# A drain of GpSimd's queue, independent scatters and a later load at the end of an attention and mixture-of-experts kernel

## The chip, the cores and the metric

The kernel runs on one core of one Trainium2 chip. The metric is the device time of one execution in microseconds (us), as the median of several runs; lower is better. The core has five engines with queues of their own: TensorE (PE, with its weight loads as PEld), VectorE (DVE), ScalarE (ACT), GpSimd (POOL) and SyncE (SP), which issues most transfers. A "q" behind an engine's name (POOLq, SPq) means instructions that its queue handles itself, such as waits on semaphores, register loads, branches and drains.

## The reference

Bucketed attention over 4 batches of 8 heads with 768 tokens of width 64 (a query sees the keys whose six sign bits agree with its own), and behind it a mixture of experts on the 3072 tokens of width 512. Each token goes to the one of 8 experts that scores highest:

```python
logits = x @ w_gate + modality_bias[modality_id]
e_idx = np.argmax(logits, axis=1)
...
for e in range(E):
    mask = e_idx == e
    h = np.maximum(x[mask] @ w1[e], 0.0)
    out[mask] = gate_w[mask, None] * (h @ w2[e])
```

Each row of `out` is thus written once, by the expert of its token.

## The kernel before

Attention runs first, over 16 pairs of heads. It leaves x in device memory (`x_d`), and a router writes, with indirect scatters on GpSimd (line 607), a table `tab` in which the tokens are sorted by expert, with their gate weights.

The experts then work in slots. A big slot (kinds "e" and "b") holds 512 tokens of one expert, in four groups of 128; a small one (kind "s") holds up to 128. The order is e0, e1, b0, b1, s1, b2, b3, s0: the last slot is a small one, and a big one precedes it. Within a slot, GpSimd gathers the tokens from `x_d` (line 770), TensorE multiplies by w1 (steps j = 0 to 3) and w2 (j = 4 to 7) with weights that SP loads and ACT and DVE split into two parts (lines 742 to 752), and at the slot's end `store` (line 849) does two things for each group of 128 tokens: ACT scales the result out of PSUM into a tile `y` (line 852; four buffers), and GpSimd scatters `y` to the rows of `out` that the table names (line 853).

The rows of a scatter are known at run time only. The framework that orders the instructions therefore takes two scatters to `out` as two writes of the same tensor, and puts a wait in front of each: GpSimd holds the next scatter until the one before it has landed.

For the case that an expert has more tokens than the eight slots hold, `conditional` follows (line 931). Every engine loads the flag `tot[0:1, 2:3]` into a register (line 941) and branches on it (line 942); with these inputs the flag is 0 and the body is skipped. An engine that skips the body raises the semaphores that the body would have raised (single event-semaphore instructions on each engine and, on GpSimd, one INC_SWDGE_SEM for those of its transfers). After that comes the framework's own end of the program, which the profile books under line 994: SP waits on the semaphores, each engine has a DRAIN, and all meet at a barrier. The kernel has no drain of its own. The program's begin is booked under line 991.

Instructions of one engine run in the order of its queue. In the slots from the third on that order is the framework's; `tc.issue_after(ins)` keeps what is inside it behind `ins` on the engine of `ins` alone, and `tc.declare_no_dep` takes the dependence between two instructions away.

Of the kernel before, what the change touches and what calls it, by code (L numbers as in the profile page):

```python
# [490 lines left out]
N = B * S  # L491
# [221 lines left out]
def experts(ctx, tc, a, x_d, tab, out, ps_x, ident, first, adds):  # L713
    nc = tc.nc
# [14 lines left out]
    def nt(s):  # L729
        return 1 if s[0] == "s" else TG  # L730
# [61 lines left out]
    def gemm1(hi, lo, xh, xl, hh, hl):  # L792
        hi = hi.rearrange("p (c f) -> p c f", c=4)
        lo = lo.rearrange("p (c f) -> p c f", c=4)
        for fb in range(2):
            fs = slice(fb * P, (fb + 1) * P)
            hps = ps_h.tile([P, TS], F32, name="hps")
            for c in range(4):
                nc.tensor.matmul(hps, lo[:, c, fs], xh[:, c], start=(c == 0), stop=False)  # L799
                nc.tensor.matmul(hps, hi[:, c, fs], xl[:, c], start=False, stop=False)  # L800
                nc.tensor.matmul(hps, hi[:, c, fs], xh[:, c], start=False, stop=(c == 3))  # L801
            th = hp.tile([P, TS], F32R, name="hh")
            tl = hp.tile([P, TS], F32R, name="hl")
            with tc.high_priority(offset=CFG["hpo"]):
                nc.scalar.activation(th, hps, AF.Relu)  # L805
                nc.vector.scalar_tensor_tensor(out=tl, in0=hps, scalar=0.0, in1=th.bitcast(F32), op0=ALU.max, op1=ALU.subtract)  # L806
            hh.append(th)
            hl.append(tl)
            if fb == 0:
                yield  # L810

    def gemm1_small(hi, lo, xh, xl):
        hi = hi.rearrange("p (c f) -> p c f", c=4)
        lo = lo.rearrange("p (c f) -> p c f", c=4)
        hps = ps_h.tile([P, TS], F32, name="hps")[:, 0:FW]
        for c in range(4):
            nc.tensor.matmul(hps, xh[:, c, 0:P], lo[:, c], start=(c == 0), stop=False)
            nc.tensor.matmul(hps, xl[:, c, 0:P], hi[:, c], start=False, stop=False)
            nc.tensor.matmul(hps, xh[:, c, 0:P], hi[:, c], start=False, stop=(c == 3))
        h = hp.tile([P, FW], F32, name="hn", bufs=2)  # L820
        nc.scalar.activation(h, hps, AF.Relu)
        return h

    def turn_small(h, hh, hl):
        tp = ps_h.tile([P, TS], F32, name="hps")[:, 0:FW]
        for fb in range(2):
            nc.tensor.transpose(tp[:, fb * P:(fb + 1) * P], h[:, fb * P:(fb + 1) * P], ident)
        th = hp.tile([P, TS], F32R, name="hh")[:, 0:FW]
        tl = hp.tile([P, TS], F32R, name="hl")[:, 0:FW]
        nc.scalar.copy(out=th, in_=tp)  # L830
        nc.vector.tensor_tensor(out=tl, in0=tp, in1=th.bitcast(F32), op=ALU.subtract)
        for fb in range(2):
            hh.append(th[:, fb * P:(fb + 1) * P])
            hl.append(tl[:, fb * P:(fb + 1) * P])

    def gemm2(j, hi, lo, hh, hl, yps):
        hi = hi.rearrange("p (c f) -> p c f", c=2)
        lo = lo.rearrange("p (c f) -> p c f", c=2)
        for fb in range(2):
            fc = (j - 4) * 2 + fb  # L840
            for g in range(len(yps)):
                gs = slice(g * P, (g + 1) * P)
                nc.tensor.matmul(yps[g], hl[fc][:, gs], hi[:, fb], start=(fc == 0), stop=False)  # L843
                nc.tensor.matmul(yps[g], hh[fc][:, gs], lo[:, fb], start=False, stop=False)  # L844
                nc.tensor.matmul(yps[g], hh[fc][:, gs], hi[:, fb], start=False, stop=(fc == 7))  # L845
            if fb == 0:
                yield

    def store(tb, yps):
        for g in range(len(yps)):  # L850
            y = yp.tile([P, DM], F32, name="y")
            nc.scalar.activation(y, yps[g], AF.Copy, scale=tb[:, g, 1:2].bitcast(F32))  # L852
            nc.gpsimd.indirect_dma_start(out=out, out_offset=bass.IndirectOffsetOnAxis(ap=tb[:, g, 0:1], axis=0), in_=y, in_offset=None,  # L853
                                         bounds_check=N - 1, oob_is_err=False)

    class Runner:


        def __init__(self):
            self.raws, self.ws, self.got, self.xs = {}, {}, {}, {}  # L860
            self.nl = self.ns = self.n = 0
            self.seq, self.order = [], []

        def extend(self, lst):
            self.order += lst
            self.seq += [(s, j) for s in lst for j in range(8)]
# [25 lines left out]
        def slot(self, k):  # L892
            s = self.order[k]
            nxt = self.order[k + 1] if k + 1 < len(self.order) else None
            for _ in self.prepare(s):
                pass
            hh, hl, h = [], [], None
            ready = self.prepare(nxt) if nxt else iter(())
            for j in range(8):
                self.ahead()  # L900
                if j == (2 if k == 1 else 0) and k > 0:
                    for s2 in self.order[k + 1:k + 1 + CFG["fd"]]:
                        self.fetch(s2)
                if j == 4:
                    yps = [ps_y.tile([P, DM], F32, name="yps") for _ in range(nt(s))]
                    if k != 1:
                        for n, _ in enumerate(ready):
                            if k == 0 and n == 0:
                                break
                hi, lo = self.ws.pop(self.n)  # L910
                if j >= 4 or nt(s) > 1:
                    for _ in gemm2(j, hi, lo, hh, hl, yps) if j >= 4 else gemm1(hi, lo, *self.xs[s], hh, hl):
                        if k == 0 and j >= 4 or k == 1 and j >= 6:
                            next(ready, None)
                        yield
                    if k == 0 and j >= 4 or k == 1 and j >= 6:
                        next(ready, None)
                else:
                    last, h = h, gemm1_small(hi, lo, *self.xs[s])
                    if last is not None:  # L920
                        turn_small(last, hh, hl)
                if j == 4 and h is not None:
                    turn_small(h, hh, hl)
                self.n += 1
                yield
            store(self.got[s][0], yps)

    def conditional(tot):
        def rest(kind, i, n, col):
            if i == n:  # L930
                return
            t = nc.values_load(tot[0:1, col:col + 1], min_val=0, max_val=16, skip_runtime_bounds_check_because="a count of slots") if i in (SURE_BIG, SURE_SML) else rest.t
            rest.t = t
            with tc.If(t > i):
                r = Runner()
                r.extend([(kind, i)])
                for _ in r.slot(0):
                    pass
                rest(kind, i + 1, n, col)

        more = nc.values_load(tot[0:1, 2:3], min_val=0, max_val=1, skip_runtime_bounds_check_because="0 or 1")  # L941
        with tc.If(more > 0):
            rest("b", SURE_BIG, NBIG, 0)
            rest("s", SURE_SML, NSML, 1)
# [5 lines left out]
def body(tc, a, out):  # L950
# [3 lines left out]
    with ExitStack() as ctx, ExitStack() as actx:  # L954
        route, early_slots, early_tables, early_tiles, late_slots, setup, latest, adds, bias = router(ctx, tc, a, x_d, tab)
        finish, finish_x, ps_x, ident = attention(ctx, actx, tc, a, x_d, route, setup, early_slots, early_tables, latest, adds, bias)
        actx.close()
        runner, tabs, conditional = experts(ctx, tc, a, x_d, tab, out, ps_x, ident, early_tiles, adds)
        r = runner()
        r.extend([("e", i) for i in range(EARLY)])  # L960
# [37 lines left out]
```

## Time and profile before

| | us |
|---|---|
| median of 3 runs (lowest, highest) | 808.18 (806.52, 808.47) |
| the profiled execution | 806.52 |
| its span, from first to last instruction | 804.5 |
| TensorE busy | 751.0 (93%) |
| DVE, ACT, POOL busy | 501.7, 413.4, 438.9 |

The profiled execution is the quickest of the three runs; 2.02 us of its time lie outside the span. Times in the rows are us from the span's start. A row of the timeline gives start, duration, engine, line and operation, and in brackets the idle time of the engine before it with what ended that. Register, branch, semaphore and drain instructions don't count as busy: a stretch at the end in which all engines show zero can still hold such instructions, and they are found by their line.

### The profile page before, as it was taken

Reading aid. Unit: us, or ns where it says so; the run is one execution under the profiler, and the core shown is the slowest. Engines: PE = TensorE matmul, PEld = TensorE weight load, DVE = VectorE, ACT = ScalarE, POOL = GpSimd, SP = SyncE. Lnnn points to the kernel's source line nnn. Section 1 sums busy time; section 2 is a strip of 40 time slices with the busy share of each in tenths; the row PEclk is TensorE's granted clock in tenths of the full one; section 3 lists DMA queues with packets and bytes.
Section 4 is the critical chain, followed back from the end, with each engine's and each line's share of the span. In section 5 each row is a group of like instructions: output and inputs, shape, how many; then the busy total and the mean of one; then the engine's idle time right before and its main releaser. Section 6 shows DMA issues by size and latency. Waiting matters only on the chain. (4 is left out here: it accounts for less than half of the span.)

```text
span 804.5 us, 11625 instructions
## 1 busy us (share of the span) xinstructions
PE 751.0 (93%) x4060; PEld 520.6 (65%) x4060; DVE 501.7 (62%) x839; ACT 413.4 (51%) x730; POOL 438.9 (55%) x321
## 2 busy tenths in 40 slices
PE   4899999999998999999899999999999999999993
PEld 2555566555565556565556546888888888888882
DVE  6787677578778669778769857744243334643420
ACT  3566676666646666666556455333343436533340
POOL 7198889778869777879866992123220103202011
PEclk9999999999999999999999999999999999999997
DMA  6665534343356543456221547475443446733310
GB/s 205 151 177 158 143 98 133 99 125 106 108 121 154 134 121 92 135 127 147 72 59 34 149 75 262 121 129 197 157 132 96 140 118 212 259 103 127 122 50 37
DMA packets 59573, 104.24 MB, mean 130 GB/s; under 512 B 9709, under 2 KB 30829, under 8 KB 59504
## 3 DMA queue, kind: packets, MB, share of 16 engines
q1 hardware_dynamic: 53424, 88.23, 39.9%
q0 software_dynamic: 4928, 13.14, 5.1%
q10 hardware_dynamic: 1152, 2.03, 0.8%
q8 instruction: 34, 0.56, 0.3%
q14 instruction: 35, 0.29, 0.2%
HBM read 59.89 MB, written 13.33 MB: 91 GB/s over the span
## 5 line engine op out<-in xcount | busy, mean ns | idle before, releaser
L295 POOL TENSOR_TENSOR sp<-sp,pb 128x768 f32<-128x768 f32 x124 | 232.2, 1895 | 14.2 <-ACT pb L292 12.9
L285 ACT ACTIVATE pb<-pss 128x512 f32<-128x512 f32 x192 | 114.1, 598 | 110.5 <-PE pss L274 101.1
L219 DVE TENSOR_REDUCE mx<-psm 128x1 f32<-128x512 f32 x192 | 130.4, 687 | 55.8 <-PE psm L217 54.2
L752 DVE TENSOR_TENSOR w<-raw,w 128x1024 fp32r<-128x1024 f32 x64 | 79.5, 1249 | 94.3 <-ACT w L750 85.5
L319 PE MATMUL psu<-pb,vt 128*64 128x512 f32 (+1 forms) x768 | 134.4, 492 | 0.0
L750 ACT CAST w<-raw 128x1024 fp32r<-128x1024 f32 x64 | 66.9, 1050 | 73.8 <-PE yps L845 62.5
L319 PEld LDWEIGHTS psu<-pb,vt 128*64 128x64 f32 x768 | 50.8, 136 | 69.1 <-issue 58.3
L295 POOL TENSOR_TENSOR sp<-pb,pb 128x768 f32<-128x768 f32 x31 | 58.9, 1921 | 54.5 <-ACT pb L292 38.1
L273 PE MATMUL pss<-a_0g 128*128 128x512 f32 x192 | 79.7, 415 | 5.4 <-ACT pb L285 3.9
L843 PE MATMUL yps<-w,hl 128*128 128x512 f32 x208 | 82.7, 398 | 0.0
L845 PE MATMUL yps<-w,hh 128*128 128x512 f32 x208 | 81.3, 391 | 0.0
L844 PE MATMUL yps<-w,hh 128*128 128x512 f32 x208 | 81.0, 389 | 0.0
L799 PE MATMUL hps<-xh,w 128*128 128x512 f32 x192 | 75.6, 394 | 0.3 <-DVE hl L806 0.2
L800 PE MATMUL hps<-xl,w 128*128 128x512 f32 x192 | 74.9, 390 | 0.5 <-DVE xl L789 0.5
L801 PE MATMUL hps<-xh,w 128*128 128x512 f32 x192 | 74.9, 390 | 0.0
L225 DVE TENSOR_REDUCE mx<-psm 128x2 f32<-128x512 f32 x96 | 66.2, 690 | 10.7 <-PE psm L223 9.0
L273 PE MATMUL pss<-a_1g 128*128 128x512 f32 x192 | 68.8, 358 | 3.7 <-ACT pb L292 3.7
L770 POOL DMA_INDIRECT xg<-x_d,tb x18 | 21.3, 1186 | 91.8 <-DMA tb<-tab 84.1
L853 POOL DMA_INDIRECT out<-y,tb x18 | 19.1, 1062 | 93.4 <-ACT y L852 48.0
L805 ACT ACTIVATE hh<-hps 128x512 fp32r<-128x512 f32 x48 | 28.7, 598 | 74.5 <-PE hps L801 73.3
L806 DVE SCALAR_TENSOR_TENSOR hl<-hps,hh 128x512 fp32r<-128x512 f32 x48 | 33.0, 688 | 52.6 <-ACT hh L805 51.9
L274 PE MATMUL pss<-b_0g 128*128 128x512 f32 x192 | 65.5, 341 | 0.0
(203 smaller groups left out, 1413.6 us busy)
## 6 DMA issues: line engine op xcount, KB each, us to landing
raw<-moe_w SPq DMA_DIRECT2D x64, 512.0 KB, 4.4
xt<-qk SPq DMA_DIRECT2D x31, 384.0 KB, 4.4
vt<-v SPq DMA_DIRECT2D x16, 384.0 KB, 7.2
a_0g<-hx SPq DMA_DIRECT2D x30, 192.0 KB, 3.5
a_1g<-hx SPq DMA_DIRECT2D x30, 192.0 KB, 3.8
x_d<-xs SPq DMA_DIRECT2D x18, 256.0 KB, 2.0
b_1g<-a_1g SPq DMA_DIRECT2D x17, 192.0 KB, 3.1
b_0g<-a_0g SPq DMA_DIRECT2D x17, 192.0 KB, 2.7
```

The lines of the kernel that those rows point to most:

```text
L219: newest[:] = [nc.vector.tensor_reduce(out=mx[:, qt + j, 1 - h, 0:1], in_=mp, axis=AX.X, op=ALU.max).ins]
L273: nc.tensor.matmul(out, t["s1"][h][:, ks], t["m1"][h][:, cs], start=True, stop=False)
L285: nc.scalar.activation(t["pb"][kt][:, h, 0:MAIN], sp, AF.Exp, scale=0.125)
L295: add = (nc.vector if h and i in CFG["spd"] else nc.gpsimd).tensor_tensor(out=t["sp"][:, h], in0=(t["pb"][0] if kt == 1 else t["sp"])[:, h ...
L319: nc.tensor.matmul(t["u"][part][64 * h:64 * h + 64, 0:w], t["v"][:, h, kt], t["pb"][kt][:, h, COLS[part]], start=False, stop=(kt == NT - 1 ...
L752: (nc.gpsimd if pool else nc.vector).tensor_tensor(out=lo, in0=r, in1=hi.bitcast(F32), op=ALU.subtract)
L799: nc.tensor.matmul(hps, lo[:, c, fs], xh[:, c], start=(c == 0), stop=False)
L800: nc.tensor.matmul(hps, hi[:, c, fs], xl[:, c], start=False, stop=False)
L801: nc.tensor.matmul(hps, hi[:, c, fs], xh[:, c], start=False, stop=(c == 3))
L843: nc.tensor.matmul(yps[g], hl[fc][:, gs], hi[:, fb], start=(fc == 0), stop=False)
L844: nc.tensor.matmul(yps[g], hh[fc][:, gs], lo[:, fb], start=False, stop=False)
L845: nc.tensor.matmul(yps[g], hh[fc][:, gs], hi[:, fb], start=False, stop=(fc == 7))
```

## The change

Three edits. Scatters to `out` from the eight sure slots are declared independent of each other, so that GpSimd no longer waits for one to land before it issues the next. In the last slot, at j = 4, a `drain` is put on GpSimd's queue behind the last scatter of the slot before; only the last scatter is still to come. And the load of the flag is kept behind the last scatter on GpSimd's queue. Runners of the conditional body are made with `sure=False` and keep their waits.

```diff
+    stored = []
+
+    def store(tb, yps, sure):
...
+            ins = nc.gpsimd.indirect_dma_start(out=out, out_offset=bass.IndirectOffsetOnAxis(ap=tb[:, g, 0:1], axis=0), in_=y, in_offset=None,
+                                               bounds_check=N - 1, oob_is_err=False).ins
+            for other in stored:
+                tc.declare_no_dep(ins, other, reason="every token is in one slot and has its own row of out")
+            if sure:
+                stored.append(ins)
...
+                if j == 4 and self.sure and k == len(self.order) - 1:
+                    with tc.issue_after(stored[-1]):
+                        nc.gpsimd.drain()
...
-                r = Runner()
+                r = Runner(False)
...
-        more = nc.values_load(tot[0:1, 2:3], min_val=0, max_val=1, skip_runtime_bounds_check_because="0 or 1")
+        with tc.issue_after(stored[-1]):
+            more = nc.values_load(tot[0:1, 2:3], min_val=0, max_val=1, skip_runtime_bounds_check_because="0 or 1")
```

## Rows read from the trace of the kernel before

**Rows 1.** The page, part 1: busy us, share and instructions of two engines.

```profile
PE 751.0 (93%) x4060; PEld 520.6 (65%) x4060; DVE 501.7 (62%) x839; ACT 413.4 (51%) x730; POOL 438.9 (55%) x321
```

**Rows 2.** Busy time by stretch: length, PE, PEld, DVE, ACT, POOL, clock, DMA share, GB/s.

```profile
540.00:790.00 250.00, 249.56 (x1185) 207.89 (x1184) 102.70 (x116) 101.66 (x146) 47.31 (x42) 1.00 0.44 141
...
793.00:794.00 1.00, 0.00 (x0) 0.00 (x0) 0.00 (x0) 0.00 (x0) 0.00 (x0) 1.00 0.48 193
794.00:795.00 1.00, 0.00 (x0) 0.00 (x0) 0.00 (x0) 0.00 (x0) 0.00 (x0) 1.00 0.08 25
...
796.00:797.00 1.00, 0.00 (x0) 0.00 (x0) 0.00 (x0) 0.00 (x0) 0.00 (x0) 0.50 0.00 0
```

**Rows 3.** Timeline of GpSimd from 770 us on: the last five scatters.

```profile
776.83 0.98 POOL L853 DMA_INDIRECT out<-y,tb  x1 [28.40 <-ACT y L852]
780.27 1.37 POOL L853 DMA_INDIRECT out<-y,tb  x1 [2.46 <-ACT hn L821]
784.04 0.98 POOL L853 DMA_INDIRECT out<-y,tb  x1 [2.39 <-ACT hh L830]
787.46 0.98 POOL L853 DMA_INDIRECT out<-y,tb  x1 [2.44 <-ACT hh L830]
791.92 0.98 POOL L853 DMA_INDIRECT out<-y,tb  x1 [3.48 <-ACT y L852]
```

**Rows 4.** The chain that ended last, in order of time: start, us, what.

```profile
787.46 3.69 DMA out<-y,tb
...
791.18 0.02 POOLq L853
...
791.72 0.50 POOLq L941
```

**Rows 5.** Line 942, 791 to 798 us: duration min/median/max in ns, starts.

```profile
L942 POOLq EVENT_SEMAPHORE  x5: 17/43/43, 795.2 to 795.5; - x5
...
L942 POOLq COMPARE_BRANCH  x1: 53/53/53, 792.3 to 792.3; - x1
L942 POOLq INC_SWDGE_SEM  x1: 1708/1708/1708, 795.6 to 795.6; - x1
```

**Rows 6.** Line 994, the end of the program, the same view.

```profile
L994 SPq EVENT_SEMAPHORE  x14: 17/28/28, 797.2 to 804.4; - x14
...
L994 POOLq DRAIN  x3: 40/107/6286, 797.3 to 804.2; - x3
```

**Rows 7.** Line 994 again, 797.5 to 803 us alone: SP's drains.

```profile
L994 SPq DRAIN  x2: 7/10/13, 798.4 to 798.4; - x2
```

**Rows 8.** Waits of SP from 500 us on: us in total, times, longest.

```profile
SPq L994 <- DMA out<-y,tb: 28.2, 1, 28.2
```

**Rows 9.** Timeline of ACT: the y of the last two slots.

```profile
775.86 1.37 ACT L852 ACTIVATE y<-yps,tb 128x512 f32<-128x512 f32 x2 [2.35 <-PE yps L845]
...
790.68 0.69 ACT L852 ACTIVATE y<-yps,tb 128x512 f32<-128x512 f32 x1 [3.76 <-PE yps L845]
```

**Rows 10.** Timeline of GpSimd, 515 us on: second of six scatters without waits.

```profile
519.86 1.00 POOL L607 DMA_INDIRECT tab<-recs,posi  x1 [0.31 <-issue]
```

**Rows 11.** The DMA view: issues from GpSimd's queue.

```profile
tab<-recs,posi POOLq DMA_INDIRECT x24
xg<-x_d,tb POOLq DMA_INDIRECT x18
out<-y,tb POOLq DMA_INDIRECT x18
...
xg<-x_d,ete POOLq DMA_INDIRECT x8
out<-y,etb POOLq DMA_INDIRECT x8
```

**Rows 12.** Line 991, the program's begin: GpSimd's queue.

```profile
L991 POOLq INC_SWDGE_SEM  x1: 27/27/27, 0.1 to 0.1; - x1
...
L991 POOLq DRAIN  x1: 188/188/188, 0.3 to 0.3; - x1
```

More of the change, by code (lines that the diff above doesn't have):

```diff
@@ L847, in gemm2 @@
                 yield
-    def store(tb, yps):
+    stored = []
+    def store(tb, yps, sure):
         for g in range(len(yps)):
@@ L852, in store, with __init__ @@
             nc.scalar.activation(y, yps[g], AF.Copy, scale=tb[:, g, 1:2].bitcast(F32))
-            nc.gpsimd.indirect_dma_start(out=out, out_offset=bass.IndirectOffsetOnAxis(ap=tb[:, g, 0:1], axis=0), in_=y, in_offset=None,
-                                         bounds_check=N - 1, oob_is_err=False)
+            ins = nc.gpsimd.indirect_dma_start(out=out, out_offset=bass.IndirectOffsetOnAxis(ap=tb[:, g, 0:1], axis=0), in_=y, in_offset=None,
[4 more added lines that the diff above has]
+                stored.append(ins)
     class Runner:
-        def __init__(self):
+        def __init__(self, sure=True):
             self.raws, self.ws, self.got, self.xs = {}, {}, {}, {}
@@ L862, in __init__ @@
             self.seq, self.order = [], []
+            self.sure = sure
         def extend(self, lst):
@@ L925, in slot @@
                 yield
-            store(self.got[s][0], yps)
+            store(self.got[s][0], yps, self.sure)
     def conditional(tot):
```

## The prediction

> **What bounds the kernel now.** I first read the page's busy times: TensorE is busy for 93% of the span [rows 1]. Next comes the table of busy time by stretch, to see whether that share is even. In the expert stage from 540 to 790 us TensorE is busy 249.56 of 250 us, so its own stream sets the time there, and GpSimd, busy 47.31 us, has room [rows 2]. The reader should see that nothing GpSimd does earlier or later in that stretch can shorten it; what is left is the tail. The last y is made on ACT from 790.68 to 791.37 [rows 9], and the span ends at 804.5, so 13.1 us pass in which no TensorE work remains.
>
> The timeline shows only one scatter in that tail [rows 3]; the rest are queue instructions, which I read by line. In order: GpSimd's wait for the scatter before ends at 791.20 and the flag's load runs 791.72 to 792.22 [rows 4]; the last scatter starts at 791.92 [rows 3]; GpSimd branches at 792.3, its next instructions come at 795.2, and INC_SWDGE_SEM takes 795.6 to 797.3 [rows 5]. Then a DRAIN of 6.29 us starts at 797.3 [rows 6] and ends at 803.59; 0.91 us of closing barrier follow. SP is done long before: its waits begin at 797.2 [rows 6, 8] and its drains stand at 798.4 [rows 7]. So the chain that sets the end is GpSimd's queue, and its largest piece is the drain.
>
> What does that drain do? No transfer is its cause: the last scatter's bytes move between 793 and 794 us, and the DMA share is 0.00 from 796 us on [rows 2]. The drain at the program's begin, with no transfer issued yet, took 0.19 us, and the two shorter ones at the end, right behind the long one, 0.04 and 0.11 us [rows 12, 6]. So a long drain comes once, the first time after 24 + 18 + 18 + 8 + 8 = 76 indirect transfers [rows 11], and those behind it are short. My reading: GpSimd's software closes the books on each transfer since the last drain, at an estimated 6.29 / 76 = 0.083 us each.
>
> A rule speaks against this. The Trainium skill, "VectorE: DVE Perf Modes", section "The DRAIN you can't avoid", says that the drains of the preamble and postamble are about 12 ns, constant, on all five engines. SP's rows (7 to 13 ns) fit it [rows 7], GpSimd's 6286 ns doesn't. By its "constant" the last drain would keep its length whatever went before; that is the first rival below, which stands on rows alone.
>
> **The change, part by part.** *Independent scatters.* They take away the waits between scatters. In the last big slot four scatters start at 776.83, 780.27, 784.04 and 787.46, about 3.5 us apart [rows 3]. All four y are ready by 775.86 + 4 x 0.69 = 778.62 [rows 9], and scatters without waits follow each other in 0.31 + 1.00 = 1.31 us, as the table's do [rows 10]. So they will start at 776.83, 778.1, 779.5 and 780.8 and leave GpSimd at 781.7. Earlier in the stage the same edit gains nothing, as TensorE's own 249.56 us cover it [rows 2]. If that cover were absent, a gather behind a waiting scatter would start some us sooner. More scatters in flight beside the weight loads cost nothing I can point to at a DMA share of 0.44 [rows 2].
>
> The last scatter no longer waits for the one before, only for its y. The first scatter of the big slot shows that case: y ends at 775.86 + 0.69 = 776.55, the scatter starts at 776.83, 0.28 later [rows 9, 3]. By that the last one starts at 791.37 + 0.28 = 791.65 in place of 791.92: **-0.27 us**.
>
> *The early drain.* It stands behind the fourth scatter on GpSimd's queue. Behind it are the last scatter, the flag's load and the branch; nobody else waits for them before the end. It has 75 transfers to close, 75 x 0.083 = 6.2 us. No row shows a drain beside other work, so I bound its end: 781.7 + 6.2 = 787.9 if it closes old transfers while the last ones land, and, with the longest landing of a scatter in the chain, 3.69 us [rows 4], 780.8 + 3.69 + 6.29 = 790.8 at the latest if it waits for all landings first. GpSimd is needed again at about 791.6. The cover is TensorE's last slot, with 0.8 to 3.7 us to spare, so the cost on the path is 0. I lean to the first end, since 71 of the 75 have landed long ago.
>
> *The load behind the last scatter.* In the trace it starts at 791.72, after the wait that stands ahead of the scatter, so it already is behind it [rows 4]; with the waits gone, the edit keeps it there. **0 us**, and at most its 0.50 us in either direction.
>
> *INC_SWDGE_SEM* isn't edited, but works on the same queue. It took 1.71 us with 76 transfers open and will meet one [rows 5, 11]. At the program's begin it took 0.03 us [rows 12]. I bound it by 0.03 and 1.71 and take 0.3, near the lower end, because the begin's state (nothing open) is nearer to one open transfer than 76 are: **-1.41 us**.
>
> *The last drain.* It has one transfer to close, so I take the program begin's 0.19 us [rows 12]. Then it is no longer the last: INC_SWDGE_SEM starts at 795.6 - 0.27 = 795.33 and ends at 795.63, GpSimd's drain ends at 795.8. SP comes late next. Its 28.2 us wait ended at 797.2, 0.1 before INC_SWDGE_SEM's end [rows 8, 6, 5] and well after the bytes had moved, so I read that instruction as its releaser. From there SP's list of waits took 1.2 us to its drains [rows 7]. So SP is through at 795.53 + 1.2 = 796.73, and 0.91 us of closing give 797.64. From INC_SWDGE_SEM's end to the span's end that is 2.01 us where it was 7.2: **-5.18 us** (797.3 to 804.5 is 7.2; rounding in the starts is about 0.05).
>
> *Sum:* -0.27 - 1.41 - 5.18 = **-6.86 us**. The profiled execution becomes 806.52 - 6.86 = 799.7 (a span of 797.64 and the same 2.02 around it). It is the lowest of three runs, 1.66 below their median; the median becomes 808.18 - 6.86 = **801.3 us**.
>
> **The rivals.** *1. The last drain stays long.* If its 6.29 us are a fixed price for ending a program that used this queue, an early drain takes nothing off it, and nothing off INC_SWDGE_SEM. Only the 0.27 remains: 807.9 us. For it: a single long drain in the trace can't prove that its length goes with a count. Against: the two behind it are short, so whatever it does once needn't be done again.
>
> *2. The scatters still stand in turn,* so that the change doesn't do what it says (another dependence, of the tiles or of the semaphores, holds them). Then the fourth leaves GpSimd at 787.46 + 0.98 = 788.44 [rows 3], the drain ends at 788.44 + 6.2 = 794.6, and the last scatter starts 3.0 to 3.2 us late, with the short end still won: 801.3 + 3.2 = 804.5 us. Against: the declaration names every pair of sure scatters, and the table's six show that the queue takes them back to back [rows 10].
>
> *3. The early drain outlasts its cover (slower).* Place: GpSimd's queue between the fourth and the last scatter. It decides from 791.6 - 784.5 = 7.1 us behind the last landing. If a drain beside running engines takes twice its length at the idle end, 12.6 us, it ends at 784.5 + 12.6 = 797.1 and holds the last scatter for 5.5 us; if moreover the last drain keeps its length, as in the first rival, the time is 807.9 + 5.5 = 813.4 us. For it: TensorE, ACT and DVE work there, none of them in the last drain. Against: both conditions are needed for a loss; with the short end won, 5.5 us are about balanced.
>
> **How the numbers follow.** The forecast, 801.3, has a chance of 0.78; the first rival 0.10, the second 0.06, the third 0.06. What a measurement of this kernel can tell from no change is about 0.3%, 2.4 us. The forecast and the second rival are faster by more (0.84), the first is within it (0.10), the third slower (0.06). The range: the forecast's own low end is INC_SWDGE_SEM at 0.03 us, 801.0, less the 1.66 us by which a run lay below the median, 799.4; its high end is INC_SWDGE_SEM at 1.71, 802.7. It reaches up to the second rival, 804.5, plus 0.3 for the run above the median, 804.8, and leaves out the other two, 0.16.
>
> **What the changed profile would show.** Right: scatters of the last big slot some 1.3 us apart; a DRAIN of about 6 us on GpSimd's queue that ends before 791.6; the last scatter at about 791.65; INC_SWDGE_SEM under 0.5 us; a last drain of 0.2 us, and SP's waits as the last list ahead of the barrier. Wrong: a long drain at the program's end (first rival), scatters 3.5 us apart (second), or a last scatter later than 792 behind a drain (third). The prediction is also wrong if the framework, with fewer dependences, orders the queues of the expert stage so that TensorE is no longer busy throughout 540 to 790 us, or if the last scatter's landing, hidden before by the branch and INC_SWDGE_SEM, comes to set the end: by the longest landing it comes at 791.65 + 3.69 = 795.34, 0.2 us ahead of SP's release.

## The result

The changed kernel takes 799.87 us (median of 6 runs, 798.16 to 803.15) where the kernel before takes 808.33 (6 runs, 806.52 to 811.33). The ratio is 0.9897 with a 95% interval from 0.9865 to 0.9929: 8.3 us less, between 5.7 and 10.9. The forecast was 801.3 us and 6.86 us less.

The profiled execution of the changed kernel took 803.15 us, the longest of its six, with a span of 801.4. It reached the last y 4 us later than the profiled execution of before and still ended 3.1 us sooner. Where the 4 us come from is told at the end; what the change does is read in the tail, from the end of the last y to the end of the span. That was 804.5 - 791.37 = 13.13 us [rows 9] and is now 801.4 - 795.40 = 6.0 us.

First part 1 of the page, which answers [rows 1]; then the timeline of ACT with the last y and that of GpSimd with the last five scatters, which answer [rows 9, 3] (start, duration, engine, line, operation, idle time before it):

```profile
PE 754.0 (94%) x4060; PEld 522.1 (65%) x4060; DVE 499.7 (62%) x839; ACT 413.5 (52%) x730; POOL 438.7 (55%) x321
...
794.71 0.69 ACT L854 ACTIVATE y<-yps,tb 128x512 f32<-128x512 f32 x1 [3.76 <-PE yps L845]
...
780.86 0.98 POOL L855 DMA_INDIRECT out<-y,tb  x1 [39.10 <-ACT y L854]
782.14 0.98 POOL L855 DMA_INDIRECT out<-y,tb  x1 [0.30 <-ACT y L854]
783.43 0.98 POOL L855 DMA_INDIRECT out<-y,tb  x1 [0.30 <-issue]
784.72 0.98 POOL L855 DMA_INDIRECT out<-y,tb  x1 [0.30 <-issue]
795.67 0.98 POOL L855 DMA_INDIRECT out<-y,tb  x1 [9.97 <-ACT y L854]
```

The four scatters follow each other in 1.29 us where they took about 3.5 [rows 3], and the last one starts 0.27 us behind its y where it took 0.55.

The queue instructions of the changed kernel, by line: the early drain (919), the flag's load (952), the branch and what follows it (953, answering [rows 5]) and the end of the program (1005, answering [rows 6, 7]). Columns: count, duration min/median/max in ns, first and last start in us. The last row is of 799.3 to 800.56 us alone.

```profile
L919 POOLq DRAIN  x1: 9245/9245/9245, 782.7 to 782.7; - x1
...
L952 POOLq TENSOR_LOAD <-tot x1: 496/496/496, 795.4 to 795.4; - x1
...
L953 POOLq EVENT_SEMAPHORE  x5: 17/43/299, 798.6 to 799.1; - x5
...
L953 POOLq COMPARE_BRANCH  x1: 58/58/58, 796.0 to 796.0; - x1
L953 POOLq INC_SWDGE_SEM  x1: 203/203/203, 799.2 to 799.2; - x1
...
L1005 SPq EVENT_SEMAPHORE  x14: 17/28/28, 799.4 to 801.3; - x14
...
L1005 POOLq DRAIN  x3: 46/107/145, 799.5 to 801.1; - x3
...
L1005 SPq DRAIN  x2: 7/10/13, 800.5 to 800.5; - x2
```

The reader should see that the long drain has left the end: the three drains of line 1005 take 0.145, 0.107 and 0.046 us where the first took 6.29 [rows 6], and INC_SWDGE_SEM takes 0.20 where it took 1.71 [rows 5]. The long bar now stands at 782.7, in front of the last y. What comes late at the end is SP's list of waits, from 799.4 to its drains at 800.5. One more row has changed: the longest of the five EVENT_SEMAPHOREs takes 0.299 us where it took 0.043 [rows 5]. In the packed trace it is the one that waits for the last scatter: that scatter's last piece landed at 798.98, and the instruction ended at 799.01.

### The profile page after: what moved, and what is told of

It reads as the page before. It is cut to its first block, busy times and chain, and to the rows that moved or that the text cites. A ratio compares the mean times of both kernels' runs of the same rounds, so it can differ in the third digit from the quotient of the medians.

```text
span 801.4 us, 11627 instructions
## 1 busy us (share of the span) xinstructions
PE 754.0 (94%) x4060; PEld 522.1 (65%) x4060; DVE 499.7 (62%) x839; ACT 413.5 (52%) x730; POOL 438.7 (55%) x321
## 4 chain that ended last, share of the span: by engine, by line
PE 65%; DVE 14%; issue 9%; ACT 5%; DMA 4%; POOL 1%; SPq 1%; POOLq 0%; ACTq 0%; DVEq 0%
PE psu L319 12%; PE pss L273 8%; PE pss L274 6%; PE hps L799 4%; PE hps L800 4%; PE hps L801 4%; PE psm L217 4%; PE yps L845 3%; PE yps L843 3%; PE yps L844 3%; PE psm L223 3%; ACT pb L285 2%; DMA x_d<-y 2%; DVE mx L219 2%; PE psx L188 2%
## 5 line engine op out<-in xcount | busy, mean ns | idle before, releaser
L274 PE MATMUL pss<-b_1g 128*128 128x512 f32 x192 | 65.7, 342 | 0.0
```

The costliest lines, as they stand in the source:

```text
L274: nc.tensor.matmul(out, t["s2"][h][:, ks], t["m2"][h][:, cs], start=False, stop=True)
```

## The experiments

The experiments ran on two chips, each beside runs of the kernel before on the same chip; ratios are to those, and times of different chips aren't compared. Scatters in turn, the drain when everything has landed, two drains, and the first 6 runs without the early drain shared one chip (before: 810.66 us, 9 runs); the 12 runs without the early drain, the drain three slots sooner and the kernel without the edge shared another (before: 811.01 us, 18 runs). Diffs are against the changed kernel. My theory: GpSimd closes each indirect transfer at a price, in the first drain that comes by, INC_SWDGE_SEM too takes longer the more of them are still open, and the early drain moves that work under TensorE's last slot. ("Closing" is a name for what takes this time; what is done in it no row shows.) Rivals: a drain at the end has a fixed price; the independence of the scatters carries the gain; the early drain isn't hidden.

**Without the early drain.**

```diff
-                if j == 4 and self.sure and k == len(self.order) - 1:
-                    with tc.issue_after(stored[-1]):
-                        nc.gpsimd.drain()
```

> The changed kernel without the early drain: independent scatters and the placed load alone. My theory (the gain is the early drain): the last drain is 6.2 to 6.3 us again, INC_SWDGE_SEM about 1.7 us, the last scatter still starts 0.3 us behind its y, and the time is 808.3 - 0.3 = 808.0 us, within 0.3% of before. The rival that the independence of the scatters carries the gain: the end stays short and the time is about 799.9 us as with the whole change.

Measured: 808.2 us, ratio 0.9979 (0.9958 to 1.0). That it comes so near to the 808.0 is chance, as the kernel before took 810.66 on this chip; by the ratio it is 1.7 us below before. Its rows of INC_SWDGE_SEM and of the end's drains on GpSimd:

```profile
L950 POOLq INC_SWDGE_SEM  x1: 1708/1708/1708, 794.7 to 794.7; - x1
...
L1002 POOLq DRAIN  x3: 40/107/6286, 796.4 to 803.3; - x3
```

Both are back to the very nanosecond, and the tail is 12.46 us. So the independence of the scatters doesn't carry the gain at the tail; without the early drain 0.7 of its 7.1 us are left. The same kernel was measured again, with more runs:

> The kernel without the early drain once more, with more rounds, beside the whole change on one chip. Its first look gave a ratio of 0.998 with an interval that touches 1. If independence is worth 0.3 to 0.7 us at the tail alone, the ratio is 0.9992 to 0.9996 and the whole change lies 6.5 to 7 us below it. If independence also shortens the stage before the tail by 1 to 2 us, the ratio is about 0.998 here too.

Measured: 807.67 us (12 runs), ratio 0.9970 (0.9947 to 0.9993), with a tail of 12.81 us. At the tail independence gives 0.3 to 0.7 us; the runs say 0.6 to 4.3 us. The interval reaches down into that, but its middle, 2.4 us, doesn't come from the tail. The distance to the whole change missed its mark as well. The same program as the whole change ran on this chip (without the edge, below): 803.58 us, 4.1 below this one by the medians where 6.5 to 7 were expected and the tails differ by 12.81 - 6.12 = 6.7. The means differ by 5.5, with a 95% interval of about 3.5 to 7.5 worked out from the single runs, so the 6.7 isn't ruled out. More on this below.

**Scatters in turn again.**

```diff
-            for other in stored:
-                tc.declare_no_dep(ins, other, reason="every token is in one slot and has its own row of out")
```

> The changed kernel with the scatters again in turn: the early drain and the placed load alone. In the kernel before the fourth scatter leaves GpSimd at 788.4; an early drain of 9.25 us, as the changed kernel shows, would end at 797.7 and hold the last scatter by 6.1 us, so about 799.9 + 6.1 = 806.0 us. By the 6.2 us of the prediction it would be held by 3.1 us: 803.0 us. The rival that the independence isn't needed (the drain is hidden in either case): 799.9 us.

Measured: 806.65 us, ratio 0.995 (0.9933 to 0.9966), 4.0 us below before. The fourth and the last scatter, the last y, and the early drain:

```profile
792.22 0.98 POOL L855 DMA_INDIRECT out<-y,tb  x1 [2.45 <-ACT hh L830]
800.27 0.98 POOL L855 DMA_INDIRECT out<-y,tb  x1 [7.06 <-issue]
...
795.44 0.69 ACT L854 ACTIVATE y<-yps,tb 128x512 f32<-128x512 f32 x1 [3.76 <-PE yps L845]
...
L917 POOLq DRAIN  x1: 7407/7407/7407, 792.0 to 792.0; - x1
```

The last y ended at 796.13, so its scatter came 4.1 us behind it, and the tail is 9.87 us: 3.9 more than with the whole change. That is neither the 6.1 us of the one estimate nor the 3.1 of the other. The drain's bar runs from 792.0 to 799.41. It begins before the fourth scatter does, and counted from that scatter's end at 793.20 it is 6.21 us, the 6.2 us of 75 transfers. Another 0.86 us pass until the last scatter starts; the kernel before has much the same step, 0.72 us from the end of the wait at 791.20 to the scatter at 791.92 [rows 4, 3]. So the early drain needs the independent scatters: without them it isn't hidden, and a good half of what it wins at the end is lost in front of it.

**The early drain when everything has landed.**

```diff
-                if j == 4 and self.sure and k == len(self.order) - 1:
-                    with tc.issue_after(stored[-1]):
+                if j == 4 and self.sure and k == len(self.order) - 2:
+                    dl = hp.tile([P, 8], F32, name="dl", bufs=1)
+                    gate = nc.gpsimd.tensor_copy(out=dl[:, 0:1], in_=hh[-1][:, 0:1].bitcast(F32)).ins
+                    with tc.issue_after(gate):
                         nc.gpsimd.drain()
```

> The early drain one slot earlier, in the last big slot, behind a one-column copy that waits for a hidden-layer tile, so that every scatter before it has landed several us earlier: 71 transfers to close, none in flight, five left for the end. If the 9.25 us of the changed kernel are 6.2 us of closing plus a wait for landings, this drain takes 71 x 0.083 = 5.9 us; if closing a transfer is dearer beside running engines (9.25 / 75 = 0.123 us), 8.7 us. The last drain with five open: 5 x 0.083 = 0.4 us if its length goes by the count, 6.3 us if it is a fixed price. Time about 799.9 + 0.3 us by the count, 807 us if fixed.

Measured: 804.49 us, ratio 0.9931 (0.9914 to 0.9947), tail 6.14 us. The condition also held in the first slot, when only two slots were known, so there were two early drains and not one, the first behind 26 transfers and the second behind 45 more. That makes two points out of one. The rows of each in its own stretch, each with the one-column copy beside it, then INC_SWDGE_SEM and the end's drains:

```profile
L921 POOLq DRAIN  x1: 2413/2413/2413, 515.3 to 515.3; - x1
...
515.28 0.18 POOL L919 COPY dl<-hh 128x1 f32<-128x1 f32 x1 [24.53 <-issue]
...
L921 POOLq DRAIN  x1: 3951/3951/3951, 759.5 to 759.5; - x1
...
759.48 0.18 POOL L919 COPY dl<-hh 128x1 f32<-128x1 f32 x1 [18.66 <-ACT hh L805]
...
L955 POOLq INC_SWDGE_SEM  x1: 288/288/288, 798.4 to 798.4; - x1
...
L1007 POOLq DRAIN  x3: 46/107/462, 798.7 to 800.3; - x3
```

In the packed trace the bars start at 515.27 and 759.47, so the copy still has to run in front of each. From the copy's end the drains take 517.68 - 515.46 = 2.22 us for 26 transfers and 763.42 - 759.66 = 3.76 for 45: 0.085 and 0.084 us a transfer. Beside running engines closing a transfer thus costs what it costs at the idle end (6.29 / 76 = 0.083), not half as much again. Bytes don't set the price either: 18 of the 26 transfers are records of the table, of 1 KB, and only 6 of the 45. Every one of them covers 128 rows, though, so a price per transfer and one per row can't be told apart. The last drain took 0.46 us where the count said 0.4 and a fixed price 6.3. By the ratio the time is 5.6 us below before (4.3 to 7.0); the tail says 7.0, the end of that interval.

**Two early drains.**

```diff
-                if j == 4 and self.sure and k == len(self.order) - 1:
+                if j == 4 and self.sure and k in (2, len(self.order) - 1):
```

> Two early drains: one in the third slot, behind the second slot's last scatter, with about 48 transfers issued before it, and the one of the change. By the count theory their lengths share the 9.25 us in proportion: about 5.9 and 3.3 us. If a drain has a fixed price beside other work, both take about 9 us. The last drain stays 0.1 to 0.2 us and the time is 799.9 us, as nothing waits for GpSimd in the third slot (if it does, the time rises by the part that is not hidden).

Measured: 802.52 us, ratio 0.9913 (0.9893 to 0.9933), tail 6.2 us, the last drain 0.135 us. By the ratio it is 7.1 us below before, by the tail 6.9. The two drains, each in its own stretch, and the fourth scatter ahead of each:

```profile
L919 POOLq DRAIN  x1: 10208/10208/10208, 585.3 to 585.3; - x1
...
587.35 1.41 POOL L855 DMA_INDIRECT out<-y,etb  x1 [0.30 <-issue]
...
L919 POOLq DRAIN  x1: 5857/5857/5857, 779.8 to 779.8; - x1
...
781.82 0.98 POOL L855 DMA_INDIRECT out<-y,tb  x1 [0.30 <-issue]
```

My two numbers missed: 10.21 us at 585.3 and 5.86 at 779.8 where I expected 5.9 and 3.3. Both bars start ahead of scatters that are still to run, so I count from the fourth scatter's end: 595.5 - 588.76 = 6.7 us for 48 transfers and 785.66 - 782.80 = 2.9 for 27. At 0.083 that is 4.0 and 2.2, so the first is 2.7 us over and the second 0.6. In the packed trace the two fourth scatters landed at 593.46 and 784.48, which is 2.0 and 1.1 us ahead of the drain's end: a wait for the landing can be part of the rest, but what fills it stays open. A fixed price of each drain it is not, since the changed kernel's drain (6.25 us from the fourth scatter's end, for 75) and the two of the last experiment agree with the count within 0.1 us.

**One early drain three slots sooner.**

```diff
-                if j == 4 and self.sure and k == len(self.order) - 1:
+                if j == 4 and self.sure and k == 4:
```

> The early drain in the fifth slot, behind the fourth slot's last scatter, and none in the last slot: 15 transfers are open at the end where it was 1, 5 and 76 so far. By a price for each open transfer (0.145 us for one and 0.082 for each more; INC_SWDGE_SEM 0.203 and 0.020) the last drain is 1.3 us and INC_SWDGE_SEM 0.48 us. A last drain of up to about 1.1 us is hidden by SP's list of waits, so the tail is 6.0 + 0.3 + 0.2 = 6.5 us. By a price that depends on the time since the last drain rather than on the count, the last drain would be nearer to that of the kernel before.

Measured, in a single execution: tail 6.56 us (the time was 800.31 us). The early drain and the fourth scatter ahead of it, then INC_SWDGE_SEM and the end's drains:

```profile
L919 POOLq DRAIN  x1: 9171/9171/9171, 674.9 to 674.9; - x1
...
676.97 0.98 POOL L855 DMA_INDIRECT out<-y,tb  x1 [0.30 <-issue]
...
L953 POOLq INC_SWDGE_SEM  x1: 488/488/488, 795.8 to 795.8; - x1
...
L1005 POOLq DRAIN  x3: 46/107/1288, 796.3 to 798.2; - x3
```

1.288 us for 1.3 expected, 0.488 for 0.48, 6.56 for 6.5. With 1, 5, 15 and 76 transfers open the last drain takes 0.145, 0.462, 1.288 and 6.286 us: 0.079, 0.083 and 0.082 us for each more. INC_SWDGE_SEM takes 0.203, 0.288, 0.488 and 1.708 us: 0.021, 0.020 and 0.020 for each more. The fixed price is out. A price by the time since the drain before isn't ruled out by these four, since the longer times go with the longer drains; the two early drains of the kernel drained when everything had landed do it: the one at 515.3 came 515 us behind the begin's drain and took 2.22 us, the one at 759.5 came 244 us behind that and took 3.76.

The early drain of this run is again longer than its count: 684.07 - 677.95 = 6.1 us from the fourth scatter's end for 61 transfers, 1.0 over. The load on the DMA engines doesn't order these rests: their share was 0.9 to 1.0 in this stretch and 0.5 to 0.6 in that of the 2.7 us.

**Without the edge on the load.**

```diff
-        with tc.issue_after(stored[-1]):
+        if True:
             more = nc.values_load(tot[0:1, 2:3], min_val=0, max_val=1, skip_runtime_bounds_check_because="0 or 1")
```

> The changed kernel without the edge that keeps the flag's load behind the last scatter. If the edge does nothing (the load already stands there, as in the kernel before), the tail from the end of the last y to the end of the span is 6.0 us as in the changed kernel, the load starts within 0.1 us of the last scatter's dispatch, and the ratio to before is 0.990. If the load moves ahead of the early drain, the branch comes 0.5 us sooner.

Without the edge the traces show the same instructions in the same order on all five engines, so the edge does nothing, and this is the whole change once more: 803.58 us (7 runs), ratio 0.9913 (0.988 to 0.9946), which is 7.1 us below before, and a tail of 6.12 us; the drain of line 919 took 9.248 us, INC_SWDGE_SEM 0.203 and the longest of the last drains 0.145 again.

## Why the prediction was right

The direction, the mechanism and nearly every term held: the tail fell by 13.13 - 6.0 = 7.1 us where the sum said 6.86, and the same program on another chip was 7.1 us below before. The 799.87 us lie in the range of 799.4 to 804.8, but near its low end: of the 8.3 us measured, 1.2 don't come from the tail and no step of the prediction explains them; the interval of 5.7 to 10.9 holds the 7.1. Step by step:

- *Scatters 1.31 us apart, the last 0.28 behind its y.* Measured 1.29 and 0.27. Right.
- *The early drain, 6.2 us from the fourth scatter's end or from the last landing.* The fourth scatter ends at 784.72 + 0.98 = 785.70 and the drain at 782.70 + 9.245 = 791.95: 6.25 us, the first end of the bounds, to which I leaned. In the packed trace the fourth scatter landed at 787.38; a drain that waited for that first and then closed all 75 would have ended at 793.6. The drain was done 3.7 us before the last scatter started; I had forecast 0.8 to 3.7 us to spare. What I hadn't said is that its bar would be 9.2 us and not 6: the queue reaches the drain while the third and the fourth scatter still have to run, and the wait for them is in the bar. Reading 9.245 / 75 as a price gave the wrong numbers for two experiments.
- *The load behind the last scatter, 0 us.* Right: it starts at 795.4, and the program without the edge is the same.
- *INC_SWDGE_SEM at 0.3 us, bounds 0.03 and 1.71.* It took 0.20. Taking the value near the lower end was right, and the reason (its time goes with the open transfers) is now four points on a line.
- *The last drain at 0.19 us, SP's list next.* The drain took 0.145. That the 0.19 of the program's begin came so near is luck: the packed trace has memsets of GpSimd until 0.45 us, inside that drain's bar from 0.31 to 0.50. The term wasn't in the sum: SP's list ran from 799.4 to 800.5, 1.1 us for the 1.2 forecast, and set the end, with 0.9 us of closing behind it.
- *The signs of being wrong.* TensorE was busy for 249.45 of the 250 us from 540 to 790, so the new order of the queues cost it nothing. The last scatter's landing, which I had 0.2 us ahead of SP's release, did come into the chain: GpSimd's semaphore instruction of 0.299 us waited for it, about 0.26 us. In the twin without the edge it is 0.392 us, in the kernel drained when everything had landed 0.207, and 0.043 in the others, where the landing came first. The sum doesn't show it because the branch took less: 796.0 to 798.6 where it was 792.3 to 795.2 [rows 5]. These two about cancel by chance.
- *The first rival, a fixed last drain,* fell to four lengths with four counts. The Trainium skill, "VectorE: DVE Perf Modes", section "The DRAIN you can't avoid", gives the drains of the end as about 12 ns, constant, on all five engines. SP's do fit (7 to 13 ns here), GpSimd's don't: 145 to 6286 ns by the count.
- *The second rival, scatters in turn,* was built as an experiment. Its price was 3.2 us over the forecast and was 3.9: the mechanism was right, and the 0.86 us between the drain's end and the next scatter's start were left out, though rows 3 and 4 show such a step.
- *The third rival, a dearer drain beside running engines,* doesn't show where every transfer had landed: 0.084 and 0.085 us for 0.083, where it needed the double. With scatters in flight the bar of the changed kernel keeps to the count too; three others ran 0.6 to 2.7 us over it, from a cause left open.

One step stays open. I said that earlier in the expert stage independent scatters gain nothing. The table gives, for each profiled execution, the time from the start of the table's last scatter to the end of the last y, which is the expert stage, and the tail behind it; all worked out from the timelines as above.

| execution | last table scatter | end of last y | expert stage | tail |
|---|---|---|---|---|
| before | 525.00 | 791.37 | 266.4 | 13.1 |
| changed | 528.75 | 795.40 | 266.7 | 6.0 |
| changed, without the edge | 524.10 | 790.68 | 266.6 | 6.1 |
| no early drain, first 6 runs | 524.60 | 791.04 | 266.4 | 12.5 |
| no early drain, 12 runs | 525.01 | 792.29 | 267.3 | 12.8 |
| scatters in turn | 529.46 | 796.13 | 266.7 | 9.9 |
| drained when landed | 527.77 | 794.46 | 266.7 | 6.1 |
| two early drains | 525.15 | 792.50 | 267.4 | 6.2 |
| drained in the fifth slot | 524.81 | 791.84 | 267.0 | 6.6 |

The expert stage isn't shorter in any of them, with scatters independent or in turn, so the traces give no place for a gain of 2.4 us without the early drain. The runs' interval allows 0.6, which the tail explains. Whether there is more couldn't be settled with single traces: the executions differ by up to 5 us ahead of the table's last scatter, where no scatter to `out` has run yet.

## What to carry to other kernels

A program that issues many indirect transfers from GpSimd pays for closing them in its last drain, here 0.08 us each, and 0.02 more in a semaphore instruction behind a skipped branch. A drain on GpSimd's queue while another engine still bounds the kernel moves that off the end, if its 0.08 us a transfer, and up to 2.7 us more as two of these kernels show, fit between the last-but-one transfer and the moment at which the last one's data are ready; waits between independent transfers on that queue eat the same gap, so they go first. Look for such tails among the queue instructions by line: the page's busy times and the chain of waits of the kernel before show nothing of these 8 us.

## What the runs showed of the hardware that I had not expected

GpSimd's drain bar begins before the work that is queued in front of it has run: 782.70, with scatters at 783.43 and 784.72 still to come. The Trainium skill, "Perfetto Trace Analysis", section "Sequencer-only Instruction (DRAIN, etc)", has the bar as the instruction's execution, without its semaphore wait; no row here shows a drain with a semaphore wait of its own, but the bar does hold the wait for the engine's own queue. Reading such a bar without the work in front of it made the price look dearer than it is, here and in the kernel drained when everything had landed.

The other is a loss of some 4 to 5 us around 260 us, in attention, which came in some executions and not in others of the same program. The stretch from 260 to 270 us in the changed kernel and in its twin without the edge (length, then busy PE, PEld, DVE, ACT, POOL, granted clock, DMA share, GB/s), and one piece of the chain of waits of the changed kernel (start, us, what):

```profile
260.00:270.00 10.00, 6.90 (x31) 3.44 (x23) 3.58 (x6) 3.40 (x6) 5.60 (x5) 0.73 0.57 119
...
260.00:270.00 10.00, 9.70 (x62) 5.12 (x62) 6.77 (x11) 6.21 (x11) 6.15 (x5) 1.00 0.58 127
...
259.86 3.10 DMA vt<-v
```

In the first TensorE stood still for 3.1 us ahead of 265.27, waiting for ACT. The granted clock was 0.73 over the stretch: full up to 264 us and 0.50 from 265 to 270, which is 1.2 GHz, the lower of the two levels. Half as many matmuls were done. The program is the same in both rows. The chain puts ACT's delay down to a load of v, but that load started at 259.86 here and at 260.24 in the twin, so it wasn't late; why ACT was stays open. Scatters in turn and the kernel drained when everything had landed show the same loss (granted clock 0.66 and 0.83 in the stretch); in the other executions of the table the granted clock is 1.00 there.
